# The head of a transformer block: centring two row tiles before the transpose, and scaling V afterwards

## The chip, the cores and the metric

The kernel runs on one core of one Trainium2 chip. The metric is the device time of one execution in microseconds (us). The kernel before takes 693.31 us, the median of 3 runs (693.14 to 693.49).

## The reference

A pre-norm transformer block on a sequence of 2048 rows of width 1024, in bf16: a layer norm without gain or bias, causal attention with 32 heads of 32 and a window of 256, a residual, a second layer norm, a SiLU feed-forward of width 3584, and a second residual.

```python
def _layernorm(x, axis=-1, eps=1e-5):
    m = jnp.mean(x, axis=axis, keepdims=True)
    v = jnp.var(x, axis=axis, keepdims=True)
    return (x - m) / jnp.sqrt(v + eps)

def _A_ref(x, wqkv, wo):                     # x: 1 x 2048 x 1024, wqkv: 1024 x 3072
    qkv = (x @ wqkv).reshape(B, S, 3, H, Dh).transpose(2, 0, 3, 1, 4)
    q, k, v = qkv[0], qkv[1], qkv[2]
    # ... scores, mask (0 <= i - j < 256), softmax, p @ v
    return o.transpose(0, 2, 1, 3).reshape(B, S, D) @ wo

h = x + _A_ref(_layernorm(x), A_wqkv, A_wo)
h2 = h + silu(_layernorm(h) @ w1) @ w2
```

Only the very first part matters here: the layer norm of the first 512 rows, and V, Q and K of these rows. A row's 1/std is one number for the row, so it can be applied to a row of x before the product with the weights, or to the row of V after it.

## The kernel before

The sequence is worked through in four blocks of 512 rows, each of four row tiles of 128 rows. TensorE needs the normed rows transposed (`lnT_b`), with the 1024 columns on the partitions in eight pieces (`kt`). In later blocks the transpose is done by DMA, off TensorE. In the first block nothing else is there to do yet, so tiles 0, 1 and 2 are transposed on TensorE (`turn_first`), through PSUM and a copy by ScalarE (ACT), and only tile 3 by DMA.

The loads at the start, all on the queue of SyncE (SP) but one; columns from 2D on are those of V:

```python
def load_x(b, j, queue=nc.sync):
    queue.dma_start(out=x_ring[(b % 2) * 4 + j], in_=x2d[(b * 4 + j) * P:(b * 4 + j + 1) * P, :])   # 256 KB

def load_wqkv(c0):                                                                                # 1 MB: 512 columns
    dst = wqk[:, :, c0:c0 + 512] if c0 < 2 * D else wv[:, :, c0 - 2 * D:c0 - 2 * D + 512]
    nc.sync.dma_start(out=dst, in_=wqkv_v[:, :, c0:c0 + 512])

load_x(0, 0)
load_wqkv(2 * D)
load_x(0, 1, nc.scalar)
load_x(0, 2)
load_wqkv(2 * D + 512)
load_x(0, 3)
load_wqkv(0)
...
for i in range(11):          # warm-up matmuls on zeros
    nc.tensor.matmul(o_ps[i % 2][:].rearrange("p a b -> p (a b)"), lhsT=warm[:, 0, 0:P], rhs=warm[:, 0, :], start=True, stop=True)
```

The layer norm's parts, on VectorE (DVE) but for the square root:

```python
def ln_half(xt, stats, c):                        # statistics of 512 columns
    nc.vector.bn_stats(out=stats[:, c, :], in_=xt[:, c * 512:(c + 1) * 512])

def ln_norm(xt, st, rs, j):                       # (x - mean) * rstd, in place
    nc.vector.tensor_scalar(out=xt, in0=xt, scalar1=st[:, j, 0:1], scalar2=rs[:, j:j + 1],
                            op0=ALU.subtract, op1=ALU.mult)

def ln_transpose(xt, dst, j):                     # a transpose by DMA
    nc.sync.dma_start_transpose(out=dst[:, :, j * P:(j + 1) * P], in_=xt)

def ln_root(st, rs, j):                           # sqrt(var + eps) on ACT; a reciprocal on DVE follows
    nc.scalar.activation(out=rs[:, j:j + 1], in_=st[:, j, 1:2], func=ACT.Sqrt, bias=eps[:], scale=1.0)

def turn_first(j, h):                             # a quarter of a tile, on TensorE
    for i in range(2):
        kt = h * 2 + i
        nc.tensor.transpose(out=tp_ps[h][:, i * P:(i + 1) * P], in_=x_ring[j][:, kt * P:(kt + 1) * P], identity=ident[:])
    nc.scalar.copy(out=lnT_b[0][:, h * 2:(h + 1) * 2, j * P:(j + 1) * P],
                   in_=tp_ps[h][:, 0:256].rearrange("p (k q) -> p k q", q=P))
```

V of one row tile and 512 columns is a group of eight matmuls into one PSUM bank, of which there are two (`acc_banks`); Q and K come in groups of eight matmuls over 512 rows:

```python
def v_group(b, j, c, copy, between=None):
    acc = next_acc()
    for kt in range(KT):
        if between:
            between(kt)
        nc.tensor.matmul(acc, lhsT=lnT_b[b % 2][:, kt, j * P:(j + 1) * P], rhs=wv[:, kt, c * 512:(c + 1) * 512],
                         start=(kt == 0), stop=(kt == KT - 1))
    copy(out=v[:, b * 4 + j, c * 16:(c + 1) * 16, 0:DH], in_=acc.rearrange("p (h d) -> p h d", d=DH))

def qk_group(b, which, g, copy, between=None):    # wqk columns which * D + g * 128, all 512 rows of lnT_b
    ...
```

The head in program order (each engine runs its own instructions in this order):

```python
ln_stats(x_ring[0], st, 0)
ln_root(st, rs, 0)
ln_half(x_ring[1], half, 0)
ln_first(x_ring[0], st, rs, 0, 4, 1)              # reciprocal, then the norm in four quarters, one on ACT
ln_stats(x_ring[1], st, 1, half)
for h in range(4):
    turn_first(0, h)
    if h == 2:
        ln_root(st, rs, 1)
ln_first(x_ring[1], st, rs, 1, 4)
ln_stats(x_ring[2], st, 2)
...                                               # tile 1's quarters are turned in and between the next two groups
v_group(0, 0, 0, lambda **args: held.append(args), turn_1)
turn_first(1, 1)
turn_first(1, 2)
v_group(0, 1, 0, act, turn_1_rest)
ln_first(x_ring[2], st, rs, 2, 1)
ln_stats(x_ring[3], st, 3)
ln_root(st, rs, 3)
ln_first(x_ring[3], st, rs, 3, 1)
ln_transpose(x_ring[3], lnT_b[0], 3)
for c0 in (D, 512, D + 512):
    load_wqkv(c0)
v_group(0, 0, 1, act)
for h in range(4):
    turn_first(2, h)
v_group(0, 1, 1, act)
v_group(0, 2, 0, act)
v_group(0, 2, 1, act)
nc.scalar.activation(out=dummy[:], in_=eps[:], func=ACT.Exp)
v_group(0, 3, 0, act)
v_group(0, 3, 1, act)
...
for j in range(4):
    load_x(1, j)
...                                               # 16 Q/K groups of block 0: Q columns 0-511, K 0-511, Q 512-, K 512-
```

Of the kernel before, what the change touches and what calls it, by code (L numbers as in the profile page):

```python
# [9 lines left out]
F32 = mybir.dt.float32  # L10
I32 = mybir.dt.int32
ACT = mybir.ActivationFunctionType
ALU = mybir.AluOpType

P = 128
# [29 lines left out]
def kernel(  # L45
# [10 lines left out]
    nc = tc.nc  # L56
# [3 lines left out]
    S, D = x2d.shape  # L60
# [4 lines left out]
    KT = D // P  # L65
# [20 lines left out]
    r_e = big.tile([P, 13312], BF16, name="r_e")  # L86
# [4 lines left out]
    tp_ps = [tp_pool.tile([P, 1024], BF16, name=f"tp{i}") for i in range(4)]  # L91
    o_ps = [ps.tile([P, 8, 64], F32, name=f"o_ps{i}") for i in range(2)]
    acc_ps = [ps.tile([P, 512], F32, name=f"acc{i}") for i in range(2)]

    def view(region, off, *dims):
        n = 1
        for d in dims:
            n *= d
        ap = region[:, off:off + n]
        if len(dims) == 2:  # L100
            return ap.rearrange("p (a b) -> p a b", b=dims[1])
        if len(dims) == 3:
            return ap.rearrange("p (a b c) -> p a b c", b=dims[1], c=dims[2])
        return ap
# [4 lines left out]
    lnT_b = [view(r_w, 24576, KT, 512), view(r_t, 0, KT, 512)]  # L109
    x_ring = [view(r_o, i * 1024, 1024) for i in range(8)]  # L110
# [17 lines left out]
    wqkv_v = A_wqkv.rearrange("(kt p) n -> p kt n", p=P)  # L128
# [5 lines left out]
    def load_x(b, j, queue=nc.sync):  # L134
        queue.dma_start(out=x_ring[(b % 2) * 4 + j], in_=x2d[(b * 4 + j) * P:(b * 4 + j + 1) * P, :])  # L135

    def load_wqkv(c0):
        dst = wqk[:, :, c0:c0 + 512] if c0 < 2 * D else wv[:, :, c0 - 2 * D:c0 - 2 * D + 512]
        nc.sync.dma_start(out=dst, in_=wqkv_v[:, :, c0:c0 + 512])

    eps = const.tile([P, 1], F32, name="eps")
    nc.vector.memset(eps[:], LN_EPS)
# [1 line left out]
    nc.scalar.activation(out=dummy[:], in_=eps[:], func=ACT.Sqrt)  # L144

    load_x(0, 0)
    load_wqkv(2 * D)
    load_x(0, 1, nc.scalar)
    load_x(0, 2)
    load_wqkv(2 * D + 512)  # L150
    load_x(0, 3)
    load_wqkv(0)

    ident = const.tile([P, P], BF16, name="ident")
    make_identity(nc, ident[:])
    warm = view(r_e, 0, 2, 512)
    nc.vector.memset(warm, 0.0)
    nc.gpsimd.memset(v[:, :, :, DH:VW], 1.0)


    for i in range(11):
        nc.tensor.matmul(o_ps[i % 2][:].rearrange("p a b -> p (a b)"), lhsT=warm[:, 0, 0:P], rhs=warm[:, 0, :], start=True, stop=True)


    def ln_half(xt, stats, c):
        nc.vector.bn_stats(out=stats[:, c, :], in_=xt[:, c * 512:(c + 1) * 512])

    def ln_stats(xt, st, j, half_done=None):
        stats = half_done
        if stats is None:  # L170
            stats = small.tile([P, 2, 6], F32, name="ln_st", tag="ln_st")
            ln_half(xt, stats, 0)
        ln_half(xt, stats, 1)
        nc.vector.bn_aggr(out=st[:, j, :], in_=stats[:])
# [18 lines left out]
    def ln_norm(xt, st, rs, j):  # L193
        nc.vector.tensor_scalar(out=xt, in0=xt, scalar1=st[:, j, 0:1], scalar2=rs[:, j:j + 1],
                                op0=ALU.subtract, op1=ALU.mult)

    def ln_transpose(xt, dst, j):
        nc.sync.dma_start_transpose(out=dst[:, :, j * P:(j + 1) * P], in_=xt)

    def ln_root(st, rs, j):  # L200
        nc.scalar.activation(out=rs[:, j:j + 1], in_=st[:, j, 1:2], func=ACT.Sqrt, bias=eps[:], scale=1.0)

    def ln_first(xt, st, rs, j, parts, on_act=0):

        if on_act:
            shift = small.tile([P, 2], F32, name="ln_shift", tag="ln_shift")
            nc.scalar.activation(out=shift[:, 0:1], in_=st[:, j, 0:1], func=ACT.Identity, scale=-1.0)
        nc.vector.reciprocal(out=rs[:, j:j + 1], in_=rs[:, j:j + 1])
        if on_act:
            nc.scalar.activation(out=shift[:, 1:2], in_=shift[:, 0:1], func=ACT.Identity, scale=rs[:, j:j + 1])  # L210
        n = 1024 // parts
        for h in range(parts):
            part = xt[:, h * n:(h + 1) * n]
            if h < parts - on_act:
                ln_norm(part, st, rs, j)
            else:
                nc.scalar.activation(out=part, in_=part, func=ACT.Identity, bias=shift[:, 1:2], scale=rs[:, j:j + 1])

    def turn_first(j, h):

        for i in range(2):
            kt = h * 2 + i
            nc.tensor.transpose(out=tp_ps[h][:, i * P:(i + 1) * P], in_=x_ring[j][:, kt * P:(kt + 1) * P], identity=ident[:])  # L223
# [196 lines left out]
    class Stream:  # L420
# [30 lines left out]

    dve, act = nc.vector.tensor_copy, nc.scalar.copy


    st, rs = ln_tiles("a")
    half = small.tile([P, 2, 6], F32, name="ln_st", tag="ln_st")
    ln_stats(x_ring[0], st, 0)
    ln_root(st, rs, 0)
    ln_half(x_ring[1], half, 0)
    ln_first(x_ring[0], st, rs, 0, 4, 1)  # L460
    ln_stats(x_ring[1], st, 1, half)
    for h in range(4):
        turn_first(0, h)
        if h == 2:
            ln_root(st, rs, 1)
    ln_first(x_ring[1], st, rs, 1, 4)
    ln_stats(x_ring[2], st, 2)

    held = []

    def turn_1(kt):
        if kt == 7:
            turn_first(1, 0)

    def turn_1_rest(kt):
        if kt == 2:
            turn_first(1, 3)
            act(**held.pop())
            ln_root(st, rs, 2)

    v_group(0, 0, 0, lambda **args: held.append(args), turn_1)
    turn_first(1, 1)
    turn_first(1, 2)
    v_group(0, 1, 0, act, turn_1_rest)
    ln_first(x_ring[2], st, rs, 2, 1)
    ln_stats(x_ring[3], st, 3)
    ln_root(st, rs, 3)
    ln_first(x_ring[3], st, rs, 3, 1)
    ln_transpose(x_ring[3], lnT_b[0], 3)
    for c0 in (D, 512, D + 512):  # L490
        load_wqkv(c0)
    v_group(0, 0, 1, act)
    for h in range(4):
        turn_first(2, h)
    v_group(0, 1, 1, act)
    v_group(0, 2, 0, act)
    v_group(0, 2, 1, act)
    nc.scalar.activation(out=dummy[:], in_=eps[:], func=ACT.Exp)
    v_group(0, 3, 0, act)
    v_group(0, 3, 1, act)  # L500

    ps_tp.__exit__(None, None, None)
    ps_sc = tc.tile_pool(name="ps_sc", bufs=1, space=bass.MemoryType.PSUM, reuse_waits="tile")
# [138 lines left out]
    for b in range(NB):  # L642
# [4 lines left out]
        for ft in range(FT):  # L647
# [8 lines left out]
            if b == 0 and 6 <= ft < 14:  # L656
                j, c = divmod(ft - 6, 2)
# [60 lines left out]
```

The softmax here doesn't subtract the row's maximum and nothing guards it: scores larger than these inputs give would overflow.

## Time and profile before

| | |
|---|---|
| time, median of 3 | 693.31 us |
| span of the profiled execution | 691.4 us |
| TensorE busy | 677.0 us, 98% |
| VectorE, ACT, GpSimd busy | 42%, 35%, 23% |
| first tile of x in place, first statistics | 4.25 us |
| first transpose on TensorE | 6.84 us |
| first V matmul | 7.92 us |
| DMA transpose of tile 3 issued | 15.32 us |
| first Q/K matmul | 22.98 us by the chain of waits |

A row of the timeline or of the page's groups gives a start, a busy time, the engine, the line of the kernel, the operation, what it writes and reads with the shapes, how many of them are merged in the row, and what ended the idle time ahead of it. PE is TensorE's matmuls (transposes too), PEld its weight loads, SPq the issuing of DMAs by SyncE. The chain of waits goes back from the last instruction to what released each step; where it names TensorE, TensorE was at work and waited for nothing. In the chain, "acc L245" are the V groups, "tp L223" the transposes on TensorE, "acc L255" the Q/K groups.

### The profile page before, as it was taken

Reading aid. Unit: us, or ns where it says so; the run is one execution under the profiler, and the core shown is the slowest. Engines: PE = TensorE matmul, PEld = TensorE weight load, DVE = VectorE, ACT = ScalarE, POOL = GpSimd, SP = SyncE. Lnnn points to the kernel's source line nnn. Section 1 sums busy time; section 2 is a strip of 40 time slices with the busy share of each in tenths; the row PEclk is TensorE's granted clock in tenths of the full one; section 3 lists DMA queues with packets and bytes.
Section 4 is the critical chain, followed back from the end, with each engine's and each line's share of the span. In section 5 each row is a group of like instructions: output and inputs, shape, how many; then the busy total and the mean of one; then the engine's idle time right before and its main releaser. Section 6 shows DMA issues by size and latency. Waiting matters only on the chain.

```text
span 691.4 us, 14107 instructions
## 1 busy us (share of the span) xinstructions
PE 677.0 (98%) x5895; PEld 331.6 (48%) x6011; DVE 290.5 (42%) x609; ACT 241.8 (35%) x463; POOL 160.4 (23%) x295
## 2 busy tenths in 40 slices
PE   8999999999999999999999999999999999999998
PEld 3444455555555555544444444444444444444445
DVE  5267646744444439534315133343133251333111
ACT  5326666766666666421310033300133100233000
POOL 1007666656666666500000000000000000000000
PEclk9999999999999999999999999999999999999999
DMA  8732242136241889971023410022300024100110
GB/s 251 251 55 78 39 80 61 26 63 183 73 131 17 241 235 281 213 277 50 12 80 111 93 39 0 1 91 69 85 0 1 17 95 95 39 1 1 30 39 24
DMA packets 76463, 60.95 MB, mean 88 GB/s; under 512 B 50288, under 2 KB 60528, under 8 KB 76400
## 3 DMA queue, kind: packets, MB, share of 16 engines
q1 hardware_dynamic: 76256, 59.78, 32.0%
q8 instruction: 47, 0.77, 0.5%
q10 hardware_dynamic: 144, 0.26, 0.1%
q14 instruction: 16, 0.13, 0.1%
HBM read 39.85 MB, written 8.39 MB: 70 GB/s over the span
## 4 chain that ended last, share of the span: by engine, by line
PE 97%; issue 1%; DMA 1%; SPq 0%; DVE 0%
PE hacc L628 19%; PE hacc L665 17%; PE acc L255 16%; PE acc L665 10%; PE acc L628 9%; PE acc L245 8%; PE acc L276 7%; PE o_ps L388 5%; PE sc L308 3%; PE hacc L276 1%; DMA r_w<-in_A_wqkv_dram 1%; PE sc L360 1%; PE sc L334 1%; PE tp L223 0%; SPq L135 0%
## 5 line engine op out<-in xcount | busy, mean ns | idle before, releaser
L378 POOL TENSOR_SCALAR_AFFINE_SELECT r_e<-r_e 128x512 bf16<-128x512 bf16 (+1 forms) x288 | 157.4, 561 | 126.6 <-ACT r_e L368 62.7
L665 PEld LDWEIGHTS <-r_a 128*128 128x128 bf16 x952 | 90.9, 98 | 103.0
L628 PEld LDWEIGHTS <-r_w 128*128 128x128 bf16 x896 | 87.4, 98 | 105.0 <-issue 0.2
L665 PE MATMUL hacc<-r_a 128*128 128x512 bf16 (+2 forms) x607 | 121.8, 359 | 0.5
L628 PE MATMUL hacc<-r_e,r_w 128*128 128x512 bf16 x444 | 99.7, 379 | 0.5
L320 ACT ACTIVATE r_e<-sc 128x768 bf16<-128x768 f32 x96 | 78.2, 814 | 48.3 <-PE sc L308 47.6
L637 ACT ACTIVATE r_n<-hacc 128x512 f32<-128x512 f32 x30 | 17.9, 597 | 178.9 <-PE hacc L628 175.5
L665 PE MATMUL acc<-r_a 128*128 128x512 bf16 x329 | 73.5, 379 | 0.4
L255 PEld LDWEIGHTS <-r_w 128*128 128x128 bf16 x512 | 44.2, 97 | 46.1 <-issue 1.0
L255 PE MATMUL acc<-r_t,r_w 128*128 128x512 bf16 x233 | 60.3, 379 | 2.4 <-issue 1.7
L257 DVE CAST r_a<-acc 128x512 bf16<-128x512 f32 x56 | 38.6, 690 | 56.6 <-PE acc L255 43.8
L255 PE MATMUL acc<-r_w 128*128 128x512 bf16 x240 | 58.0, 379 | 1.5 <-issue 0.9
L388 PEld LDWEIGHTS <-r_e 128*128 128x128 bf16 x1440 | 47.4, 96 | 17.9
L276 PE MATMUL acc<-r_o,r_a 128*128 128x512 bf16 x188 | 49.5, 379 | 1.9 <-issue 1.3
L628 PE MATMUL acc<-r_e,r_w 128*128 128x512 bf16 x213 | 48.9, 379 | 0.3
L388 PE MATMUL o_ps<-r_a,r_e 128*128 128x33 bf16 x1440 | 48.1, 178 | 0.1
L321 ACT ACTIVATE r_e<-sc 128x256 bf16<-128x256 f32 x96 | 37.6, 392 | 0.0
L680 DVE SCALAR_TENSOR_TENSOR r_t<-hacc,r_t 128x512 bf16<-128x512 f32 (+2 forms) x22 | 14.0, 635 | 55.2 <-PE hacc L665 53.8
L680 DVE SCALAR_TENSOR_TENSOR r_t<-acc,r_t 128x512 bf16<-128x512 f32 x12 | 8.3, 692 | 64.2 <-PE acc L665 58.8
L638 DVE SCALAR_TENSOR_TENSOR r_a<-r_n,hacc 128x512 bf16<-128x512 f32 x30 | 20.6, 688 | 33.0 <-ACT r_n L637 33.0
L628 PE MATMUL hacc<-r_a,r_w 128*128 128x512 bf16 x139 | 32.6, 379 | 0.3
L276 PEld LDWEIGHTS <-r_a 128*128 128x128 bf16 x256 | 21.8, 97 | 22.3
(79 smaller groups left out, 532.5 us busy)
## 6 DMA issues: line engine op xcount, KB each, us to landing
r_w<-in_B_w_dram SPq DMA_DIRECT2D x8, 896.0 KB, 5.2
r_a<-in_B_w_dram SPq DMA_DIRECT2D x7, 1024.0 KB, 7.5
r_w<-in_A_wqkv_dram SPq DMA_DIRECT2D x6, 1024.0 KB, 9.3
h_dram<-r_t SPq DMA_DIRECT2D x16, 256.0 KB, 2.5
r_t<-h_dram SPq DMA_DIRECT2D x16, 256.0 KB, 2.9
out_dram<-r_t SPq DMA_DIRECT2D x31, 128.0 KB, 1.7
r_o<-in_A_x_dram SPq DMA_DIRECT2D x15, 256.0 KB, 4.2
r_e<-h_dram SPq DMA_DIRECT2D x3, 1024.0 KB, 5.7
```

The source lines that it names most:

```text
L245: nc.tensor.matmul(acc, lhsT=lnT_b[b % 2][:, kt, j * P:(j + 1) * P], rhs=wv[:, kt, c * 512:(c + 1) * 512], start=(kt == 0), stop=(kt == KT ...
L255: nc.tensor.matmul(acc, lhsT=wqk[:, kt, col0:col0 + P], rhs=lnT_b[b % 2][:, kt, :], start=(kt == 0), stop=(kt == KT - 1))
L257: copy(out=(qT, kT)[which][b][:, g, :], in_=acc)
L276: nc.tensor.matmul(acc, lhsT=qT[b][:, g, j * P:(j + 1) * P], rhs=wo[:, g, c * 512:(c + 1) * 512], start=(g == 0), stop=(g == G - 1))
L308: nc.tensor.matmul(sc[hh // 2][half * 64:half * 64 + 64, hh % 2, col:col + qb - qa], lhsT=kT[t // 4][r0:r0 + DH, g, k0:k0 + 64], rhs=qT[b] ...
L320: nc.scalar.activation(out=tri[:, :, :, 64:256], in_=both, func=ACT.Exp, scale=scale)
L321: nc.scalar.activation(out=e[:, 1024:1280].rearrange("p (h q) -> p h q", q=P), in_=bank[:, :, 192:320], func=ACT.Exp, scale=scale)
L378: nc.gpsimd.affine_select(out=dst, in_=src, pattern=[[0, n] for n in dst.shape[1:-1]] + [[sgn, P]], compare_op=ALU.is_ge if upper else ALU ...
L388: nc.tensor.matmul(o_ps[pair][:, qt * 2 + hh, 0:VW], lhsT=chunk_of(i, bank, piece, pair, hh), rhs=v[:, b * 4 + kt, g * 4 + pair * 2 + hh, ...
L628: nc.tensor.matmul(acc, lhsT=w1[:, kt, ft * P:(ft + 1) * P], rhs=ln2T[b][:, kt, :], start=(kt == 0), stop=(kt == KT - 1))
L665: nc.tensor.matmul(acc[:, 0:c1 - c0], lhsT=gT[:, ft, j * P:(j + 1) * P], rhs=w2[ft // 4][:, ft % 4, c0:c1], start=(ft == 0), stop=(ft == F ...
L680: nc.vector.scalar_tensor_tensor(out=t_out[j % 2][:, c0:c1], in0=acc[:, 0:c1 - c0], scalar=0.5, in1=t_in[j % 2][:, c0:c1], op0=ALU.mult, o ...
```

## The change

Tiles 0 and 1 go to TensorE before their variance is known. Only the mean is taken, half of it by ACT with a running sum and half by VectorE; the centred copy (`x_mid`) is transposed on TensorE and multiplied with V's weights. The products stay in PSUM until 1/std is there, and ACT applies it as the scale of the copy out of PSUM. That takes four PSUM banks: the two output banks of the attention are lent to V. Q and K need the fully normed rows with the 512 rows in one operand, so tiles 0 and 1 are normed in full later, and transposed by DMA into the same place, over the centred ones. Tile 2's transpose moves from TensorE to DMA as well.

The first half of V's weights is loaded in four parts and the second in two, so that a matmul can begin when the columns' first rows are there. Both first x tiles go on SP's queue, ahead of the weights. The load of the first Q columns moves from the start to behind the four DMA transposes. The aim is to let TensorE start on V sooner, and to take the square root, the reciprocal and the second half of the statistics off its way.

```diff
-    def load_wqkv(c0):
+    def load_wqkv(c0, parts=1):
         dst = wqk[:, :, c0:c0 + 512] if c0 < 2 * D else wv[:, :, c0 - 2 * D:c0 - 2 * D + 512]
-        nc.sync.dma_start(out=dst, in_=wqkv_v[:, :, c0:c0 + 512])
+        n = KT // parts
+        for k in range(0, KT, n):
+            nc.sync.dma_start(out=dst[:, k:k + n, :], in_=wqkv_v[:, k:k + n, c0:c0 + 512])
...
     load_x(0, 0)
-    load_wqkv(2 * D)
-    load_x(0, 1, nc.scalar)
+    load_x(0, 1)
+    load_wqkv(2 * D, 4)
     load_x(0, 2)
-    load_wqkv(2 * D + 512)
+    load_wqkv(2 * D + 512, 2)
     load_x(0, 3)
-    load_wqkv(0)
...
-    for i in range(11):
-        nc.tensor.matmul(... lhsT=warm[:, 0, 0:P], rhs=warm[:, 0, :] ...)
+    wide = bass.AP(tensor=warm.tensor, offset=warm.offset, ap=[warm.ap[0], [0, 4], warm.ap[1]])
+    for i in range(10):
+        nc.tensor.matmul(... lhsT=warm, rhs=wide ...)
...                                               # turn_first reads x_mid[j] in place of x_ring[j]
+    def mean_parts(j):
+        nc.scalar.activation(out=scrap, in_=x_ring[j][:, 512:1024], func=ACT.Identity, scale=-1.0 / D, accum_out=mean_b[:, j:j + 1])
+        ln_half(x_ring[j], halves[j], 0)
+        nc.vector.tensor_scalar(out=mean_a[:, j:j + 1], in0=halves[j][:, 0, 1:2], scalar1=halves[j][:, 0, 4:5], scalar2=-0.25,
+                                op0=ALU.add, op1=ALU.mult)
+
+    def center(j):
+        for h in range(4):
+            nc.vector.tensor_scalar(out=x_mid[j][:, h * 256:(h + 1) * 256], in0=x_ring[j][:, h * 256:(h + 1) * 256],
+                                    scalar1=mean_a[:, j:j + 1], scalar2=mean_b[:, j:j + 1], op0=ALU.add, op1=ALU.add)
...
+    def scaled(j):
+        args = held.pop(0)
+        nc.scalar.activation(func=ACT.Identity, scale=rs[:, j:j + 1], **args)
...
+    acc_banks += [o[:].rearrange("p a b -> p (a b)") for o in o_ps]
+    mean_parts(0)
+    center(0)
+    mean_parts(1)
+    center(1)
+    turn_first(0, 0)
+    turn_first(0, 1)
+    v_group(0, 0, 0, hold, place({1: (0, 2), 3: (0, 3), 5: (1, 0), 7: (1, 1)}))
+    turn_first(1, 2)
+    turn_first(1, 3)
+    ln_stats(x_ring[2], st, 2)
+    ln_root(st, rs, 2)
+    ln_stats(x_ring[0], st, 0, halves[0])
+    ln_root(st, rs, 0)
+    ln_recip(rs, 2)
+    ln_norm(x_ring[2], st, rs, 2)
+    ln_transpose(x_ring[2], lnT_b[0], 2)
+    v_group(0, 1, 0, hold)
+    v_group(0, 0, 1, hold)
+    ln_recip(rs, 0)
+    scaled(0)
+    ln_stats(x_ring[1], st, 1, halves[1])
+    ln_root(st, rs, 1)
+    ln_norm(x_ring[0], st, rs, 0)
+    ln_transpose(x_ring[0], lnT_b[0], 0)
+    ln_recip(rs, 1)
+    scaled(1)
+    scaled(0)
+    ln_stats(x_ring[3], st, 3)
+    ln_root(st, rs, 3)
+    v_group(0, 1, 1, hold)
+    ln_recip(rs, 3)
+    ln_norm(x_ring[3], st, rs, 3)
+    ln_transpose(x_ring[3], lnT_b[0], 3)
+    ln_norm(x_ring[1], st, rs, 1)
+    ln_transpose(x_ring[1], lnT_b[0], 1)
+    scaled(1)
+    for c0 in (0, D, 512, D + 512):
+        load_wqkv(c0)
     v_group(0, 2, 0, act)
     v_group(0, 2, 1, act)
     nc.scalar.activation(out=dummy[:], in_=eps[:], func=ACT.Exp)
     v_group(0, 3, 0, act)
     v_group(0, 3, 1, act)
+    del acc_banks[2:]
```

More of the change, by code (lines that the diff above doesn't have):

```diff
@@ L135, in load_x @@
         queue.dma_start(out=x_ring[(b % 2) * 4 + j], in_=x2d[(b * 4 + j) * P:(b * 4 + j + 1) * P, :])
-    def load_wqkv(c0):
+    def load_wqkv(c0, parts=1):
         dst = wqk[:, :, c0:c0 + 512] if c0 < 2 * D else wv[:, :, c0 - 2 * D:c0 - 2 * D + 512]
-        nc.sync.dma_start(out=dst, in_=wqkv_v[:, :, c0:c0 + 512])
+        n = KT // parts
+        for k in range(0, KT, n):
+            nc.sync.dma_start(out=dst[:, k:k + n, :], in_=wqkv_v[:, k:k + n, c0:c0 + 512])
+    warm = view(r_e, 0, P)
+    nc.vector.memset(warm, 0.0)
     eps = const.tile([P, 1], F32, name="eps")
@@ L146 @@
     load_x(0, 0)
-    load_wqkv(2 * D)
-    load_x(0, 1, nc.scalar)
+    load_x(0, 1)
+    load_wqkv(2 * D, 4)
     load_x(0, 2)
-    load_wqkv(2 * D + 512)
+    load_wqkv(2 * D + 512, 2)
     load_x(0, 3)
-    load_wqkv(0)
     ident = const.tile([P, P], BF16, name="ident")
     make_identity(nc, ident[:])
-    warm = view(r_e, 0, 2, 512)
-    nc.vector.memset(warm, 0.0)
     nc.gpsimd.memset(v[:, :, :, DH:VW], 1.0)
-    for i in range(11):
-        nc.tensor.matmul(o_ps[i % 2][:].rearrange("p a b -> p (a b)"), lhsT=warm[:, 0, 0:P], rhs=warm[:, 0, :], start=True, stop=True)
+    wide = bass.AP(tensor=warm.tensor, offset=warm.offset, ap=[warm.ap[0], [0, 4], warm.ap[1]])
+    for i in range(10):
+        nc.tensor.matmul(o_ps[i % 2][:].rearrange("p (a c) b -> p a (c b)", c=2), lhsT=warm, rhs=wide, start=True, stop=True)
     def ln_half(xt, stats, c):
@@ L201, in ln_root, with ln_recip @@
         nc.scalar.activation(out=rs[:, j:j + 1], in_=st[:, j, 1:2], func=ACT.Sqrt, bias=eps[:], scale=1.0)
[L203 to L207, printed above, removed]
+    def ln_recip(rs, j):
         nc.vector.reciprocal(out=rs[:, j:j + 1], in_=rs[:, j:j + 1])
[L209 to L217, printed above, removed]
     def turn_first(j, h):
@@ L222, in turn_first @@
             kt = h * 2 + i
-            nc.tensor.transpose(out=tp_ps[h][:, i * P:(i + 1) * P], in_=x_ring[j][:, kt * P:(kt + 1) * P], identity=ident[:])
+            nc.tensor.transpose(out=tp_ps[h][:, i * P:(i + 1) * P], in_=x_mid[j][:, kt * P:(kt + 1) * P], identity=ident[:])
         nc.scalar.copy(out=lnT_b[0][:, h * 2:(h + 1) * 2, j * P:(j + 1) * P],
@@ L455 @@
     st, rs = ln_tiles("a")
-    half = small.tile([P, 2, 6], F32, name="ln_st", tag="ln_st")
-    ln_stats(x_ring[0], st, 0)
-    ln_root(st, rs, 0)
[L459 to L485, printed above, removed]
+    x_mid = [view(r_e, 1024 + 1024 * j, 1024) for j in range(2)]
+    scrap = view(r_e, 3072, 512)
+    mean_a = small.tile([P, 2], F32, name="mean_a")
+    mean_b = small.tile([P, 2], F32, name="mean_b")
@@ new lines @@
+    halves = [small.tile([P, 2, 6], F32, name=f"ln_h{j}") for j in range(2)]
+    def mean_parts(j):
[7 more added lines that the diff above has]
+                                    scalar1=mean_a[:, j:j + 1], scalar2=mean_b[:, j:j + 1], op0=ALU.add, op1=ALU.add)
@@ new lines, with hold, place @@
+    held = []
+    def hold(**args):
+        held.append(args)
+    def scaled(j):
+        args = held.pop(0)
+        nc.scalar.activation(func=ACT.Identity, scale=rs[:, j:j + 1], **args)
+    def place(at):
+        return lambda kt: turn_first(*at[kt]) if kt in at else None
+    acc_banks += [o[:].rearrange("p a b -> p (a b)") for o in o_ps]
[6 more added lines that the diff above has]
+    v_group(0, 0, 0, hold, place({1: (0, 2), 3: (0, 3), 5: (1, 0), 7: (1, 1)}))
@@ L486 @@
+    ln_recip(rs, 1)
+    scaled(1)
+    scaled(0)
     ln_stats(x_ring[3], st, 3)
     ln_root(st, rs, 3)
-    ln_first(x_ring[3], st, rs, 3, 1)
+    v_group(0, 1, 1, hold)
+    ln_recip(rs, 3)
+    ln_norm(x_ring[3], st, rs, 3)
     ln_transpose(x_ring[3], lnT_b[0], 3)
-    for c0 in (D, 512, D + 512):
+    ln_norm(x_ring[1], st, rs, 1)
+    ln_transpose(x_ring[1], lnT_b[0], 1)
+    scaled(1)
+    for c0 in (0, D, 512, D + 512):
         load_wqkv(c0)
-    v_group(0, 0, 1, act)
-    for h in range(4):
-        turn_first(2, h)
@@ L495 @@
-    v_group(0, 1, 1, act)
     v_group(0, 2, 0, act)
```

## The prediction

> **What bounds the kernel now.** I read four views in this order: the page's engine table and its chain that ended last, the same chain in order of time over the first 60 us, the timeline of the first 25 us, and the short stretches with their DMA columns. The page first:
>
> ```profile
> span 691.4 us, 14107 instructions
> ...
> PE 677.0 (98%) x5895; PEld 331.6 (48%) x6011; DVE 290.5 (42%) x609; ACT 241.8 (35%) x463; POOL 160.4 (23%) x295
> ...
> PE 97%; issue 1%; DMA 1%; SPq 0%; DVE 0%
> ```
>
> TensorE is busy for 98% of the span and carries 97% of the chain; the only DMA on the chain is 1%. So a change to the head of the kernel is worth exactly what it moves the moment at which TensorE goes into its unbroken run. The chain in order of time shows where that is:
>
> ```profile
> 1.26 6.61 DMA r_w<-in_A_wqkv_dram
> 7.88 0.04 issue
> 7.92 1.67 PE acc L245 x7
> ...
> 10.88 2.59 PE acc L245 x12
> ...
> 13.90 0.45 PE tp L223 x8
> 14.35 8.63 PE acc L245 x40
> 22.98 0.22 PE acc L255
> ```
>
> The reader is to see two things. V cannot start before 7.87 us, when the first half of the V weights, one 1 MB transfer, has landed (1.26 + 6.61). From 7.92 to 22.98 TensorE then does 64 V matmuls (0.216 us each in the last group, 8.63/40) and the transposes of tiles 1 and 2 without a real gap; at 22.98 the Q/K groups begin, and nothing after them waits for the head. My reference point is therefore 22.98: whatever the change makes of the start of Q/K is what it makes of the kernel.
>
> **What the Trainium skill says.** DMA: Bandwidth & Descriptors, section Issuing engines are not separate DMA queues, says that DMAs started by different engines run on the same 16 DMA engines and interleave. The trace agrees: the tile loaded from ACT's queue (issued 0.97, 3.9 us to landing) shares the first microseconds with the tile and weights of SP's queue, so putting both tiles on SP saves no bandwidth; it only orders them. Advanced Engine Details and Errata, section X-Bar Transpose (TRN2), says that transposing DMAs are as fast as regular ones, at 350 to 400 GB/s. The trace does not agree: the lone transpose of tile 3 shows 185 to 224 GB/s with all the DMA engines busy (below), against 377 to 385 for plain loads. VectorE: DVE Perf Modes, section on the fixed extra latency of SBUF-source operations, says that many small instructions pay that cost each. The trace agrees: one 128x1024 normalisation takes 0.55 us, four of 128x256 take 1.12.
>
> **The change part by part.** These are the rows that I price with:
>
> ```profile
> 4.25 1.29 DVE L166 BATCH_NORM_STATS2 ln_st<-r_o 128x6 f32<-128x512 bf16 x2 [2.76 <-DMA r_o<-in_A_x_dram]
> 8.70 1.12 DVE L194 TENSOR_SCALAR r_o<-r_o,st_a,rs_a 128x256 bf16<-128x256 bf16 x4
> 12.67 1.28 DVE L166 BATCH_NORM_STATS2 ln_st<-r_o 128x6 f32<-128x512 bf16 x2
> 14.22 0.29 ACT L201 ACTIVATE rs_a<-st_a,eps 128x1 f32<-128x1 f32 x1 [1.42 <-DVE st_a L174]
> 14.75 0.55 DVE L194 TENSOR_SCALAR r_o<-r_o,st_a,rs_a 128x1024 bf16<-128x1024 bf16 x1
> 15.32 1.34 SPq L198 DMA_TRANSPOSE r_w<-r_o  x1
> 16.71 2.68 SPq L139 DMA_DIRECT2D r_w<-in_A_wqkv_dram  x3
> ```
>
> They give: statistics of a half 0.65, a full tile 1.3, aggregate and its dependence about 0.25, square root on ACT with both handovers 0.6, reciprocal 0.2, one norm 0.5; from the start of tile 3's statistics to the issue of its transpose 15.32 - 12.67 = 2.65. A DMA transpose holds SP for 1.35 and lands 3.2 after its issue (the DMA issues view). The 1 MB load issued at 16.71 behind it landed 5.5 later.
>
> *Step 1, the earlier start of V.* Tile 0 landed 4.2 before (0.81 + 3.4) and I keep that. Statistics of half a tile (0.65), while ACT sums the other half, then the mean (0.2), then four centring steps of about 0.26 pitch: the centred tile 0 is ready from 5.4 to 6.2. Root, reciprocal and the second half's statistics are off the path. The second tile does the same from 6.2, and its centred quarters come at 7.4, 7.7, 7.9 and 8.2. Quarters of the V weights: the same bytes stand ahead of the last one as before, so it lands at about 7.9, the others at steps of 256 KB / 365 GB/s = 0.7: 5.7, 6.4, 7.1. So the first V matmul goes at about 6.0 (transpose 0.1 each, ACT copy 0.3), and the first group is paced by the quarters and by tile 1's centring, ending at about 8.5. Then V(tile 1, first half) 8.6 to 10.4; V(tile 0, second half) needs the later 512 KB parts, about 9.9 and 11.5 (the whole landed at 11.55 before), so ends near 12.4; V(tile 1, second half) ends near 14.1. Before, this point was 14.35 + 8 x 0.216 = 16.1, so **2.0 us are won here**, of which 0.45 is the eight transposes of tile 2 that leave TensorE (13.90 above).
>
> *Step 2, the wait for tile 2.* Tile 2 landed at 8.5 before (1.72 + 6.8), and as many bytes precede it now. VectorE then does its statistics (1.3), the second half and aggregate of tile 0 (0.9, hiding the root), the reciprocal and the norm: the transpose is issued at about 11.6 and lands at 14.8. V of tile 2 is wanted at 14.1: **0.7 lost**. It ends at 14.8 + 3.45 = 18.3.
>
> *Step 3, the wait for tile 3.* VectorE goes on: reciprocal, second half of tile 1's statistics (1.1), norm of tile 0 (0.5), reciprocal, and then the 2.65 of tile 3. It comes to 13.15 for the start of tile 3's statistics, 15.8 for its transpose, 19.0 for its landing: **0.7 lost**, V ends at 19.0 + 3.45 = 22.5. Were that all, Q/K would start 0.5 us earlier than before.
>
> *Step 4, the first Q/K weights.* Before, the load of Q's first columns was issued at 5.43 and landed at 15.2, long before its use. Now it stands on SP's queue behind all four transposes. Norm of tile 1 ends at 16.2, its transpose gets onto SP at 17.2 (15.8 + 1.35), the load at 18.55. With the 5.5 us of the row above it lands at **24.1**. These stretches show why I don't take less:
>
> ```profile
> 17.25:17.50 0.25, 0.25 (x3) 0.13 (x2) 0.00 (x0) 0.00 (x0) 0.00 (x0) 1.00 1.13 207
> 18.25:18.50 0.25, 0.25 (x2) 0.10 (x1) 0.00 (x0) 0.18 (x1) 0.00 (x0) 1.00 0.72 78
> 18.75:19.00 0.25, 0.25 (x3) 0.13 (x2) 0.00 (x0) 0.00 (x0) 0.00 (x0) 1.00 0.89 299
> ```
>
> The columns after the stretch are sum, PE, PEld, DVE, ACT, POOL, clock, DMA share, GB/s. The load was issued at 16.71, yet its 300 and more GB/s begin only at 18.75, when the transpose ahead has landed (15.32 + 3.2). In the changed kernel the transpose of tile 1 lands at 20.4 to 21.4 (3.2 alone; 4.2 was the median of four in a row), and landing of the load is 22.2 - 18.75 = 3.45 later: 23.9 to 24.9. I take 24.3 for the start of Q/K. The whole head: -2.0 + 0.7 + 0.7 + 1.8 (22.5 to 24.3) gives about +1.2 to +1.3.
>
> *What lies beside the path.* The V evacuations on ACT (0.59 each) only change their scale and their order; they are held until reciprocals exist at about 11.5, and the two output banks borrowed for V make four, so none of the first four groups waits for a bank. The ten warm-up matmuls end before 6. The x tiles of the next block follow 4 MB of weights instead of 3: 20.7 + 11.5 + 1.1 = about 33.3 for the first; VectorE wants it after the Q/K group that ends near 31 and must be back by 36: no wait of TensorE.
>
> **The rivals.** First, the change wins what it is meant to. For it: step 1 is solid, 22.5 is before 22.98, and a load alone needs only about 1.1 us (0.81 to about 1.9 for the first bytes) + 2.9 + 0.4 from its issue: 18.55 + 4.4 = 22.95. If the load overlaps the transpose ahead of it, the time is 692.8 to 693.3. Against it: the 18.75 above. Second, VectorE's chain is longer than I count: each handover between ACT and VectorE on the way to four norms may add 0.1 to 0.2, tile 2 may land later, and four transposes in a row may take over 4 us each. That adds up to 1: 695.3. For it: one transpose of the next block took 4.8 to land. Third, the later x tiles stall VectorE and with it the Q/K evacuations: one stall of 0.5 to 1 us, 695. Against it: two groups of slack, as counted. Fourth, two or three short gaps let the array's clock fall: TensorE: Matmul & The Clock Gate, section What's actually happening, gives about 3.4 us of idling for that, and my gaps are 0.7, 0.7 and 1.8; the page of before shows a full granted clock throughout, and no run here shows a fall.
>
> **Range and chances.** 693.31 + 1.25 = 694.6; the first rival I give about three in ten, so I shade to **694.3 us**. The range is from the first rival with some luck, 692.4, to the second, 695.6. Two per cent would be 13.9 us, almost the whole V stage: faster by that 0.01, within 0.98, slower 0.01.
>
> **What would show it.** Step 1: the first V matmul at 6.0 and a first group that ends near 8.5. Step 2: a wait of V for a DMA-transposed tile near 14. Step 3: the same near 18.5. Step 4: the chain goes through a weight load, not through TensorE, just before the first Q/K matmul, at about 24.3, and the load's issue is near 18.5, after the fourth transpose. If the first Q/K matmul comes before 22.9 I am wrong in step 4; if it comes right after V's last matmul but late, I am wrong in step 2 or 3; if Q/K starts where I say and the total differs, something past 25 us has moved, and the third rival is the place to look.

## The result, and the profile after

The changed kernel takes 695.65 us (median of 4 runs, 695.21 to 696.41) against 693.24 for the kernel before (4 runs, 693.14 to 693.49): a ratio of 1.0036, 95% interval 1.0022 to 1.0051. It is slower by 2.4 us, where 1.0 had been predicted, and just beyond the upper end of the range. The page of the changed kernel, its head and the shares of the chain by engine:

```profile
span 693.6 us, 14104 instructions
...
PE 677.4 (98%) x5887; PEld 330.7 (48%) x6002; DVE 291.0 (42%) x614; ACT 242.2 (35%) x460; POOL 160.4 (23%) x295
...
PE 93%; DMA 3%; issue 1%; SPq 1%; DVE 1%; ACT 0%
```

TensorE is as busy as before (677.4 against 677.0), yet its share of the chain fell from 97% to 93%. The 4% that went, about 28 us, can't all be lost time, since the kernel lost 2.4; it means that the early part of the chain now runs through other work while TensorE was busy beside it. The chain in order of time says through what:

```profile
15.31 1.92 PE acc L235 x8
...
21.31 2.81 SPq L141
...
24.16 10.82 DMA r_o<-in_A_x_dram
...
35.01 1.30 DVE ln_st L169 x2
...
36.54 0.57 DVE r_a L247
...
37.15 0.81 PE acc L245 x3
```

L141 is now the load of Q/K/V weights, L235 the V groups, L245 the Q/K groups, L169 the statistics, L247 the copy of a Q/K bank. Before, the chain lay on TensorE from 7.92 on. Now it leaves TensorE in the middle of V, follows the issue of the weight loads on SP to 24.12, and then 10.8 us of one transfer: the first x tile of the next block, which lands at 34.98. VectorE's statistics of that tile follow, then the copy of a Q/K bank that stands behind them in VectorE's program, and only then TensorE, at 37.15. Between 24 and 35 TensorE isn't on the chain at all. The timeline shows its gaps (start, busy time, engine, line, what, and in brackets the idle time ahead and its releaser):

```profile
15.31 1.90 PE L235 MATMUL acc<-r_w 128*128 128x512 bf16 x8 [0.68 <-DMA r_w<-r_o]
19.20 1.90 PE L235 MATMUL o_ps<-r_w 128*128 128x512 bf16 x8 [0.26 <-DMA r_w<-r_o]
24.13 12.26 PE L245 MATMUL acc<-r_w 128*128 128x512 bf16 x55 [1.31 <-DMA r_w<-in_A_wqkv_dram]
37.15 3.18 PE L245 MATMUL acc<-r_w 128*128 128x512 bf16 x13 [0.76 <-DVE r_a L247]
```

Four waits: two of V for DMA transposes, one of Q/K for its first weights, one for the bank. Q/K begins at 24.13. The timeline of before has it at 22.82 (the chain counts a matmul from the end of the one ahead of it, and has 22.98):

```profile
22.82 27.79 PE L255 MATMUL acc<-r_w 128*128 128x512 bf16 x125
```

So Q/K is 1.31 late. In the timelines the attention's first matmul, which ends the head, comes at 52.78 against 50.54, 2.24 later. The other 0.93 arose between them, at the bank: Q/K has no wait in it before, and one of 0.76 after. The span is 2.2 us longer: nothing of note was lost or won behind the head.

### The profile page after: what moved, and what is told of

Read it like the earlier page. It is cut to its first block, busy times and chain, and to the rows that moved or that the text cites. A ratio compares the mean times of both kernels' runs of the same rounds, so it can differ in the third digit from the quotient of the medians.

```text
span 693.6 us, 14104 instructions
## 1 busy us (share of the span) xinstructions
PE 677.4 (98%) x5887; PEld 330.7 (48%) x6002; DVE 291.0 (42%) x614; ACT 242.2 (35%) x460; POOL 160.4 (23%) x295
## 4 chain that ended last, share of the span: by engine, by line
PE 93%; DMA 3%; issue 1%; SPq 1%; DVE 1%; ACT 0%
PE hacc L648 18%; PE hacc L685 17%; PE acc L245 14%; PE acc L685 10%; PE acc L648 9%; PE acc L266 7%; PE acc L235 6%; PE o_ps L378 5%; PE sc L298 3%; DMA r_o<-in_A_x_dram 2%; PE hacc L266 1%; SPq L141 1%; PE sc L350 1%; PE sc L324 1%; DMA r_w<-r_o 0%
## 5 line engine op out<-in xcount | busy, mean ns | idle before, releaser
L245 PEld LDWEIGHTS <-r_w 128*128 128x128 bf16 x512 | 44.1, 97 | 48.6 <-issue 2.0
L245 PE MATMUL acc<-r_t,r_w 128*128 128x512 bf16 x232 | 60.1, 379 | 2.0 <-issue 1.0
L245 PE MATMUL acc<-r_w 128*128 128x512 bf16 x240 | 58.2, 379 | 3.5 <-DMA r_w<-in_A_wqkv_dram 1.3
L247 DVE CAST r_a<-acc 128x512 bf16<-128x512 f32 x56 | 38.5, 688 | 55.0 <-PE acc L245 42.1
```

The source lines that it names most:

```text
L245: nc.tensor.matmul(acc, lhsT=wqk[:, kt, col0:col0 + P], rhs=lnT_b[b % 2][:, kt, :], start=(kt == 0), stop=(kt == KT - 1))
L247: copy(out=(qT, kT)[which][b][:, g, :], in_=acc)
```

## The experiments

Theory A: the x tiles decide. They land so late that VectorE stalls on them, the bank copy behind the stall is late, and whatever TensorE did before is caught up on that moment. Theory B: the waits for the Q weights and for the bank are two losses that add up. All times stand against the kernel before, run beside them: 693.32 in the first two groups of runs, 693.09 in the third (ACT's order mended; V weights whole and TensorE kept busy), 693.13 in the last (Q weights early; the change again).

### First Q weights in quarters

```diff
     for c0 in (0, D, 512, D + 512):
-        load_wqkv(c0)
+        load_wqkv(c0, 1 if c0 else 4)
```

> The changed kernel with the first Q weights loaded in four quarters, so that Q/K need not wait for the whole 1 MB. Theory A (the x tiles of the next block decide: they land at 35.0, VectorE's statistics wait for them and hold up the copy of a Q/K bank, and TensorE catches up on that moment whatever it did before): Q/K starts at about 22.8 instead of 24.1, but TensorE's gap near 37 grows from 0.8 to about 2 us, and the time stays at 695.6 within 0.3. Theory B (the two waits of TensorE, 1.15 us for the Q weights and 1.1 us at the bank, add up, each with its own cause): 694.4.

Measured: 695.98 us (1.0042, interval 1.0029 to 1.0056), no better than the change itself. The timeline of TensorE in this run:

```profile
22.53 1.03 PE L245 MATMUL acc<-r_w 128*128 128x512 bf16 x4
24.05 0.60 PE L245 MATMUL acc<-r_w 128*128 128x512 bf16 x2 [0.49 <-DMA r_w<-in_A_wqkv_dram]
25.50 10.96 PE L245 MATMUL acc<-r_w 128*128 128x512 bf16 x50 [0.85 <-DMA r_w<-in_A_wqkv_dram]
37.30 15.70 PE L245 MATMUL acc<-r_w 128*128 128x512 bf16 x72 [0.83 <-DVE r_a L247]
```

Q/K did begin 1.6 us sooner, and the time stayed, as A has it. But the gap at the bank didn't grow to 2 us; Q/K lost its lead to waits for the later quarters. The third and the fourth were there only for 24.05 and 25.50, the last of them 1.4 later than the undivided 1 MB (24.13). The fourth quarter was also issued 1.6 later, at 20.08 where the whole was issued at 18.48, because each issue holds SP for about 0.5; whether that alone makes it late isn't shown. So this run alone doesn't separate A from B; the one that does is the next.

### Q weights early, x tiles still late

The first Q weights go back to the start, and in their old place the same 1 MB is loaded into a buffer that isn't read before it is written anew, so that as much stands ahead of the x tiles as in the change. The change itself ran beside it.

```diff
     load_x(0, 3)
+    load_wqkv(0)
...
-    for c0 in (0, D, 512, D + 512):
+    nc.sync.dma_start(out=lnT_b[1], in_=wqkv_v[:, :, 0:512])
+    for c0 in (D, 512, D + 512):
         load_wqkv(c0)
```

> The changed kernel with the first Q weights loaded at the start, and in their old place a load of the same 1 MB into a buffer that nobody reads, so that four loads still stand ahead of the x tiles. Q/K then starts at about 23.4 instead of 24.1 without a wait for weights, and the x tiles still land at about 35. Theory A (the wait for the Q weights lies off the chain, the x tiles decide): the gap of TensorE near 37 grows from 0.8 to about 1.5, TensorE goes on at 37.1 to 37.3 as before, time 695.6 within 0.3. Theory B (the two waits add): the gap stays at 0.8, TensorE goes on near 36.4, time 694.9.

> The changed kernel itself, beside the run with the Q weights early, so that the two are compared on one chip: 695.6, TensorE goes on at about 37.2 after the bank wait.

Measured: 695.75 us (1.0036, interval 1.0023 to 1.0048) with the Q weights early, 695.44 (1.0032, interval 1.0019 to 1.0044) for the change again. TensorE with the Q weights early, and below it the change again:

```profile
22.25 1.89 PE L236 MATMUL acc<-r_w 128*128 128x512 bf16 x8
23.97 12.25 PE L246 MATMUL acc<-r_w 128*128 128x512 bf16 x56
37.69 2.53 PE L246 MATMUL acc<-r_w 128*128 128x512 bf16 x11 [1.47 <-DVE r_a L248]
```

```profile
24.43 12.26 PE L245 MATMUL acc<-r_w 128*128 128x512 bf16 x56 [1.32 <-DMA r_w<-in_A_wqkv_dram]
37.43 2.75 PE L245 MATMUL acc<-r_w 128*128 128x512 bf16 x12 [0.74 <-DVE r_a L247]
```

Q/K follows V with no wait for weights, half a microsecond sooner (23.97 against 24.43), and loses it all at the bank: the gap doubles from 0.74 to 1.47, TensorE goes on at 37.69 instead of 37.43, because the first x tile lands 0.26 later (35.53 against 35.27), and the two medians lie within each other's intervals. The five runs with the Q weights early spread from 694.43 to 696.48, so it is the trace more than the median that decides. It shows theory A: the x tile decides when TensorE goes on, and the wait for the Q weights costs nothing as long as it does.

### x tiles before the last two weight loads

```diff
-    for c0 in (0, D, 512, D + 512):
-        load_wqkv(c0)
+    load_wqkv(0)
+    load_wqkv(D)
+    for j in range(4):
+        load_x(1, j)
+    load_wqkv(512)
+    load_wqkv(D + 512)
```

> The changed kernel with the four x tiles of the next block loaded before the last two of the four Q/K weight loads instead of behind all four. Theory A: the x tiles land near 29 to 30, the gap near 37 is gone, Q/K still starts at 24.1, time 694.5. Theory B: the same 694.5, since one of two added waits goes. A third possibility (the weights that are put back are now missed): a new wait of Q/K for weights near 38 us, time 695 or more; they should land near 31 to 35, so I don't expect it.

Measured: 694.62 us (1.0021, interval 1.0014 to 1.0027), 1.0 less than the change; 16 of its 21 runs took less than the fastest of the change's ten (695.05). Q/K, in the timeline, is now one run of 128 matmuls:

```profile
24.00 27.80 PE L245 MATMUL acc<-r_w 128*128 128x512 bf16 x128 [1.51 <-DMA r_w<-in_A_wqkv_dram]
```

The first x tile, issued at 19.49, lands 9.2 later, at 28.7 instead of 35.0; the gap at the bank is gone, and the weights put back are nowhere missed. What remains, 1.3 us, is the late start of Q/K: 1.2 at its first matmul (24.00 for 22.82), and still 1.2 at the attention's first (51.73 for 50.54).

### The bank copy ahead of the statistics

```diff
-                for _ in range(0 if n < 4 else 1 if n < 10 else 2):
+                for _ in range(0 if n < 5 else 1 if n < 10 else 2):
```

> The changed kernel with the next block's statistics begun one Q/K group later in VectorE's program, behind the bank copy of the sixth group instead of ahead of it; no load is touched. Theory A (late x tiles stall VectorE, and through its program order the bank copy): the x tiles still land at about 35.0, but the copy no longer stands behind them, the gap of TensorE near 37 is gone, Q/K still starts at 24.1, time 694.6 as with the x tiles moved forward. Rival: the gap is not a matter of VectorE's order (weights, or the DMA load itself): no change, 695.6.

Measured: 694.8 us (1.0021, interval 1.0013 to 1.0029). The x tile lands at 35.4, as late as ever, and TensorE has no gap. VectorE's timeline in this run shows the exchange:

```profile
34.95 0.69 DVE L247 CAST r_a<-acc 128x512 bf16<-128x512 f32 x1 [2.76 <-PE acc L245]
35.56 1.28 DVE L169 BATCH_NORM_STATS2 ln_st<-r_o 128x6 f32<-128x512 bf16 x2
```

The copy goes at 34.95, when its Q/K group is done, in place of 36.45. So the late tile by itself costs no time on TensorE; it costs what stands behind its statistics in VectorE's program. With the run before, this shows the second term of the loss: about 1 us, from the landing of x and VectorE's order together.

### Both edits together

This takes the first Q weights in quarters, and the order of loads of the run with the x tiles moved forward.

> Both edits together: first Q weights in quarters, x tiles before the last two weight loads. Theory A and B agree: Q/K starts at about 22.8 with no gap behind it, time 693.0 to 693.2, level with the kernel before. Set against the two single runs it tells A from B: with A the first edit is worth nothing alone and 1.3 on top of the second; with B it is worth 1.2 both times.

Measured: 695.11 us (1.0028, interval 1.0018 to 1.0038); neither theory's number. In the profile Q/K starts at 22.38, but after four matmuls waits for the third and fourth quarters, the last of which lands at 24.71. The attention's first matmul comes at 51.20, 0.5 ahead of the run with the x order alone. But the profiled execution was the fastest of eight (694.46; median 695.11), so it doesn't show what the median lost. Even in it the lead was gone at the end: its span is 692.6 us, for 692.5 with the x order alone. A wait of 0.3 us near 287 for a transpose of the second norm, which the run with the x order alone doesn't have, is part of that; the rest stays open. The second expectation, that the quarters are worth 1.3 once the x tiles are out of the way, failed with the quarters' late landing; what an earlier start of Q/K is worth then is seen with the Q load at the start, below.

### One part of the change in the kernel before

```diff
     load_x(0, 3)
-    load_wqkv(0)
...
-    for c0 in (D, 512, D + 512):
+    for c0 in (0, D, 512, D + 512):
         load_wqkv(c0)
```

> The kernel before with one part of the change alone: the load of the first Q weights is moved from the start to behind the DMA transpose of tile 3, ahead of the other three. Theory A: the Q weights land at about 22.2, just in time for Q/K at 22.98, but the x tiles land at about 33.4 instead of 30.4, and the bank copy is late by 0.4 to 0.8 us: 693.6 to 694.1. Theory B: the Q load is in time, so nothing is lost: 693.2.

Measured: 693.93 us (1.0008, interval 0.9999 to 1.0016). Its interval just touches no difference; the trace decides. The chain of this run:

```profile
22.34 10.82 DMA r_o<-in_A_x_dram
...
33.18 1.30 DVE ln_st L165 x2
...
34.70 0.57 DVE r_a L256
...
35.31 15.70 PE acc L254 x72
```

With nothing of the centring in it, the kernel before shows the same chain as soon as a fourth weight load stands ahead of the x tiles: landing at 33.2, statistics, copy, TensorE. The Q weights themselves are in time there (issued 16.6, landing 5.5 later, for a Q/K that starts at 22.71). So the move of that load alone makes the x tiles late, by 2.7 us (33.15 for the 30.45 of before). In the changed kernel they land 4.5 late; the other 1.8 goes with the loads' issue, which begins 1.9 later there (18.48 for 16.60) because four DMA transposes stand ahead of it in place of one. That share wasn't tested by itself.

### The Q load at the start again

To the run with the x tiles moved forward this adds:

```diff
     load_x(0, 3)
+    load_wqkv(0)
...
-    load_wqkv(0)
     load_wqkv(D)
```

> The changed kernel with the first Q weights loaded at the start again, behind the x tiles, and the next block's x tiles ahead of the last two weight loads, so that only the place of the Q load differs from the run with the x tiles moved forward. Theory A (DMA work on one queue is served nearly in order): the 1 MB takes the DMA engines from 11.5 to 14.4, the transpose of tile 2 issued at 11.8 lands at about 17 instead of 15, V waits 2.3 us there instead of 0.7, Q/K starts at 23.5 to 24: 694.2 to 694.6, nothing won by it. Rival (the transpose gets its share beside the load): tile 2 lands by 15.5, V ends at 22.7, Q/K follows at once: 693.2.

Measured: 693.83 us (1.0008, interval 1.0002 to 1.0015), 0.8 under the same kernel with the load behind the transposes. The timeline shows the exchange of waits:

```profile
16.47 1.90 PE L236 MATMUL acc<-r_w 128*128 128x512 bf16 x8 [1.80 <-DMA r_w<-r_o]
...
23.39 27.79 PE L246 MATMUL acc<-r_w 128*128 128x512 bf16 x128
```

Tile 2's transpose lands 4.5 us after its issue at 11.89, 1.1 later than in the changed kernel, and V waits 1.8 us for it. But nothing waits after that, and Q/K starts 0.6 sooner (23.39 for 24.00). The result lies between the two expectations: the wait is nearer A's 2.3, and the time is under A's 694.2 and over the rival's 693.2. So the move of the Q load, which clears the way for tile 2, cost more than it gave even with the x tiles out of the way.

### Tile 2 on TensorE, and ACT's order

To that, tile 2 is transposed on TensorE between V's matmuls, and tile 3 is normed and sent before tiles 0 and 1:

```diff
-    ln_transpose(x_ring[2], lnT_b[0], 2)
...
-    v_group(0, 1, 1, hold)
+    v_group(0, 1, 1, hold, place({1: (2, 0), 3: (2, 1), 5: (2, 2), 7: (2, 3)}))
...                                    # ln_norm and ln_transpose of 3, then of 0, then of 1
```

> A version meant to beat both: as the run with the Q load at the start, with tile 2 transposed on TensorE again between the matmuls of V(tile 1, second half), and VectorE's order changed so that tile 3 is normed and sent to its DMA transpose before tiles 0 and 1. Theory A: no V group waits for a DMA transpose, V ends near 22.0, the transposes of tiles 0 and 1 land by 21.4 and Q/K starts at 22.0 to 22.3: 692.3 to 692.7. Rival (the transposes of tiles 0 and 1 come too late, or landing times scatter): Q/K at 22.6 to 23, 693.0 to 693.3.

Measured: 693.66 us (1.0005, interval 0.9997 to 1.0013). Both expectations missed it: Q/K starts at 23.32. V still waits 1.18 for tile 3, because I had put the square root of tile 3 behind the copies of tile 2 in ACT's program: it runs at 15.41 instead of 14.2, and the transpose is issued at 16.41. The next run mends this: the copies begin in V(tile 0, second half), and the root of tile 1 follows that of tile 3.

```diff
-    v_group(0, 0, 1, hold)
     ln_recip(rs, 0)
     scaled(0)
+    v_group(0, 0, 1, hold, place({5: (2, 0), 7: (2, 1)}))
...
-    v_group(0, 1, 1, hold, place({1: (2, 0), 3: (2, 1), 5: (2, 2), 7: (2, 3)}))
+    v_group(0, 1, 1, hold, place({1: (2, 2), 3: (2, 3)}))
```

> The version with tile 2 on TensorE, with ACT's order mended: in the run before, the square root of tile 3 stood in ACT's program behind the four copies of tile 2, which end at 15.4, so tile 3's transpose was issued at 16.4 and V waited 1.2 us for it. Here the copies begin one V group earlier and the root comes at about 14.2. Theory A: the transpose is issued at 15.3, lands at 18.6, V hardly waits, Q/K starts at 22.1 to 22.3 against 23.3: 692.3 to 692.7, below the kernel before. Rival (the transposes of tiles 0 and 1 then hold up Q/K, or the gain is lost further on): 693.0 or more.

Measured: 693.02 us against 693.09 (0.9997, interval 0.9989 to 1.0005): level with the kernel before, not ahead of it. Q/K starts at 22.77 by the chain, 0.2 sooner than before. Two steps fell short: the second half of V's weights lands only for 12.11, and tile 3's transpose is issued at 15.64, for a root that ran at 14.53 behind the last copy.

### V weights whole, and TensorE kept busy

The two runs here start from the version with tile 2 on TensorE, as it was before ACT's order was mended.

```diff
-    load_wqkv(2 * D, 4)
+    load_wqkv(2 * D)
...
-    load_wqkv(2 * D + 512, 2)
+    load_wqkv(2 * D + 512)
```

> That version with each half of V's weights loaded in one piece again. If the early start of V is worth what step 1 of the prediction says, the first V matmul moves from 6.2 to 8.0 and V ends 0.8 to 1.0 us later (the first group no longer overlaps tile 1's centring, and 2 transposes of tile 1 still fall between): 693.1 to 693.6. If the parts' start is swallowed by later waits, within 0.2 of the version with parts.

Measured: 696.95 us (1.0047, interval 1.0034 to 1.0061), 3.3 more than with parts (693.66), over three times what I expected. The first V matmuls of this run:

```profile
9.01 0.46 PE L236 MATMUL acc<-r_w 128*128 128x512 bf16 x1 [3.10 <-DMA r_w<-in_A_wqkv_dram]
...
9.48 1.06 PE L236 MATMUL acc<-r_w 128*128 128x512 bf16 x2
```

The weights land at 8.97, a microsecond later than the 7.87 of before, and after 3.1 us of idling the matmuls take about 0.43 each in place of 0.216, until 12.5. The granted clock, the third column from the right in the view of stretches, agrees: it is 0.52 here:

```profile
9.00:12.50 3.50, 3.49 (x14) 1.68 (x14) 2.26 (x5) 1.12 (x3) 0.00 (x0) 0.52 1.09 360
```

To see whether the idling does that, 14 matmuls on zeros went ahead of the first V matmul; they compute nothing that is used.

```diff
     turn_first(0, 1)
+    for i in range(14):
+        nc.tensor.matmul(acc_banks[2 + i % 2]..., lhsT=warm, rhs=wide, start=True, stop=True)
     v_group(0, 0, 0, hold, ...)
```

> The version with whole V weights, with 14 matmuls on zeros put between tile 0's first transposes and the first V matmul, so that TensorE doesn't idle from 5.8 to 9.0; they compute nothing that is used. In that run the first V matmuls took 0.43 us each until 12.5, twice the usual. If idling let the array's clock fall, they now take 0.22 from 9.0 on, the first four groups end 1.6 to 1.9 us earlier, and the time is 695.1 to 695.4, against 696.95. If the slow matmuls had another cause (the weights just landed, the centring), nothing changes.

Measured: 696.12 us (1.0038, interval 1.0024 to 1.0052). The time is above what I expected, and its five runs (694.80 to 697.73) overlap with the five without the zeros (695.15 to 697.75), so a gain in time isn't shown. The durations are what I expected:

```profile
11.00 0.38 PE L236 MATMUL acc<-r_w 128*128 128x512 bf16 x1 [2.26 <-DMA r_w<-in_A_wqkv_dram]
...
11.32 0.59 PE L236 MATMUL acc<-r_w 128*128 128x512 bf16 x2
```

The matmuls run at full rate from the first (0.38 for one and 0.59 for two, so 0.21 for the second), and the granted clock stays at 1.00. The weights had just landed here too, and tile 1's steps on VectorE stood beside V as before, so those two causes fall away: the slow rate followed from the idling. That is one execution of each, and the idling was shortened from 3.10 to 2.26 us, not removed. The profiled execution is the slowest of the five; in it the 1 MB landed at 11.0, 2 us later than without the zeros, which takes the gain away. Why it landed so late stays open. What the parts alone are worth, apart from clock and scatter, these two runs don't give.

## Why the prediction was right or wrong

**Step 1, the earlier start of V: right in kind, a little too good.** The first V matmul comes at 6.21 (6.0 said), and the fourth group ends at 14.63 for 16.1 before, 1.5 us ahead for the 2.0 predicted. The centred tile 0 came on time; V(tile 0, second half) idled some 0.3 for its last weights, which landed at 11.84, and the fourth group began only at 12.74.

**Steps 2 and 3: right in kind.** 0.68 was lost for tile 2 (0.7 said) and 0.26 for tile 3 (0.7 said; V stood later, so there was less to wait for). The two errors, step 1 too good and step 3 too dear, nearly cancel in the end of V, and that is luck. But the start of Q/K doesn't test these steps: it waits for its weights, whatever V did.

**Step 4, the first Q weights: right.** Issue at 18.48 (18.55 said), and Q/K at 24.13 for 24.3. This put the first rival aside: the load's bytes came only behind the transpose ahead of it (155 GB/s from 19 to 20 us, 381 from 21 to 22; the transpose landed at 20.40). What I got wrong here is its worth: in the changed kernel this wait is off the chain, which passes by way of the x tile, and taking it away won nothing. It is felt only once the x tiles are out of the way: then the late start of Q/K is the 1.3 us that remain, and the load at the start wins 0.8 of it.

**The step that failed** is in the part on what lies beside the path: the x tiles "20.7 + 11.5 + 1.1 = about 33.3 for the first", and so "no wait of TensorE". With it fell the premise that whatever the change makes of the start of Q/K is what it makes of the kernel. The slack was counted well: VectorE had to be back by about 36, and TensorE was through with the other bank at 36.4. The landing was the error, 34.98 in place of 33.3, and in it the term of 11.5 us for four weights, which is 4.2 MB at 365 GB/s. From the last transpose's landing (20.40, for 20.7) to the fourth weight's (21.31 + 13.0 = 34.3) it took 13.9; the x tile followed 0.7 behind. From 34.98 the statistics (1.3), the aggregate and the copy end at 37.1, and TensorE waited 0.76.

The bytes did not flow that much more slowly than I said. These are two stretches of the changed kernel (DMA share and GB/s last):

```profile
20.00:35.00 15.00, 13.64 (x64) 6.04 (x63) 1.38 (x2) 3.98 (x7) 0.00 (x0) 1.00 1.06 347
35.00:36.00 1.00, 1.00 (x6) 0.42 (x5) 0.99 (x2) 0.00 (x0) 0.00 (x0) 1.00 0.09 33
```

347 GB/s over 15 us is 5.2 MB: the four weights (4.2) and nearly all of the four tiles (1.05). So when the first tile landed, almost everything was moved; yet the other three landed only at 35.6, 36.3 and 36.9, one after another. From 35.5 to 36 the DMA share is 0.06, a sixteenth, at 25 GB/s; a sixteenth of a tile, 16 KB, takes 0.65 us at that rate, and that is the step between these landings. I read this as one of the 16 DMA engines trailing the others by about 2 us, with every landing waiting for it. Why one trails isn't shown. The Trainium skill, DMA: Bandwidth & Descriptors, section Queues, rings and completion order, says that completion is not in order per issuing engine, since a transfer is split over rings of up to 16 engines. The trace agrees with the split; out of order nothing came here, as all these landings keep the order of issue.

The trace of before had the answer. Its first x tile landed behind three weights:

```profile
r_o<-in_A_x_dram SPq DMA_DIRECT2D x1, 256.0 KB, 11.0
```

Issued at 19.43, it landed at 30.45, where my sum would have given 18.75 + 8.6 + 1.1 = 28.5; the same tail of 0.06 and 25 GB/s follows. One more weight at the 3.0 us that lie between the landings of the second and the third there (26.8 and 29.8), and a last transpose that lands 1.9 later, make 35.3 of it.

The third rival thus took place, "0.5 to 1 us, 695"; I had set it aside on a landing that came 1.7 late. Set against before, the loss of 2.24 at the end of the head splits into 1.31 of late Q/K and 0.93 at the bank; but the split is one of place, not of cause: with the Q weights early the second share grows as the first shrinks. The runs with the x tiles moved and with the statistics moved took the cause of the second away, and with it 1.0 and 0.85.

**Clock: right for the change.** Its gaps of at most 1.3 us on TensorE brought no fall. The version with whole V weights idled for 3.1 us and lost half its rate: its granted clock is 1.00 from 5.76 to 9.17 and 0.50 from there to 12.58, 3.41 us. The Trainium skill, TensorE: Matmul & The Clock Gate, section What's actually happening, puts the idle window at about 3.4 us. The trace agrees with that length. In this execution the stretch ahead of the fall was not idle throughout: TensorE was busy for 0.30 us of its 3.41.

## What to carry to other kernels

A load that is moved back in a queue delays not only its own reader: look up what else stands behind it, and whose program waits for that. Where an engine that frees PSUM banks also takes statistics of freshly loaded data, place the copy that TensorE needs ahead of the statistics that can wait. Price a landing by one that a trace shows behind loads of the same kind, not by bytes over a peak rate: the trace of before gives 35.3 for the first x tile, the sum of bytes 33.3, and 34.98 was measured. A wait seen on the bounding engine isn't worth its length as long as a later wait is set by another chain.

## What the runs showed of the hardware that wasn't expected

- A part of a load can land later than the whole would have: the last quarter of the first Q weights landed at 25.5, the undivided 1 MB at 24.1, with other loads behind both (its issue came 1.6 later, too).
- The same 1 MB of V weights, issued at 1.72 in two kernels with the same loads in the same order, landed 7.2 us later in one execution and 9.2 in the other.
- In the kernel before and in the changed one the last x tiles landed up to 2 us after nearly all bytes were moved, 0.65 us apart, with the DMA share at 0.06.
- The times with the x tiles moved forward scatter more: 693.85 to 696.24 in 21 runs, against 693.02 to 693.65 in the 36 runs of the kernel before beside them. In another group of 41 runs of the kernel before, one took 695.30 and the others at most 694.10.
